# Fused attention and two feed-forward layers on one core: parameters loaded first, GpSimd's data work moved to VectorE and ScalarE, fewer row-sum additions ahead of the matmul

## The chip, the cores and the metric

The kernel runs on one core of one Trainium2 chip. The metric is the device time of one execution in microseconds. The median of three runs before is 496.93 us (496.86 to 497.22).

## The reference

Attention for 2 batches, 12 heads, 448 positions and head size 64, with a soft cap on the scores, followed by two token-wise layers on 896 tokens of width 768:

```python
scores = cap * np.tanh(scale * (q @ k.T) / cap)          # per batch and head
attn = np.exp(scores - scores.max(-1, keepdims=True))
attn = attn / (attn.sum(-1, keepdims=True) + 1e-09)
x = (attn @ v)                                           # then laid out as 896 x 768

h = x @ w_in                                             # 768 -> 2048
P = a[0] + a[1]*h + a[2]*h*h + a[3]*h*h*h
Q = 1.0 + abs(b[0])*abs(h) + abs(b[1])*h*h
x = (P / (Q + 1e-06)) @ w_out                            # 2048 -> 768

h = np.maximum(np.maximum(x @ w1, x @ w2), x @ w3)       # three 768 x 768
out = h @ w_out2                                         # 768 x 768
```

All weights arrive as 64-bit floating-point numbers. The kernel reads their two 32-bit words and makes 32-bit floats of them itself.

## The kernel before, in words

The work runs in stages that overlap at their borders. In the attention stage (about 4 to 94 us) there are six double pairs `d`, each of four heads (two pairs of heads, index `r`). For each double pair TensorE makes seven score tiles: three whole blocks of 128 keys for each `r` (call `scores(d, 0..5)`, line 629), and one tile for the left-over 64 keys of both pairs (`scores(d, 6)`, line 637, which is `scores(d, 2 * NFULL)`). ScalarE takes the tanh of each tile (lines 651 and 654), with a factor `qscale` computed from the parameters, and then the exponential (line 658). TensorE multiplies the exponentials with `v` (lines 682 and 701). For the row sums, VectorE first adds the key blocks of one `r` together (line 723; `ADDED[d]` says how many additions there are, and with 3 it also adds the left-over block on 64 partitions, line 731), and TensorE multiplies what is left with a matrix of ones (line 755). The reciprocals travel through memory and scale the attention output (lines 797 to 805), which is split into a high and a low part.

Every later matmul is done three times: high weight by high data, high by low, low by high. Lines 825, 927, 1075 and 1183 are the matmuls of the first layer up, the first layer down, the second layer (a seven-product scheme with sums of weight blocks made at line 525) and the last one.

Each weight is decoded from its 64-bit words in `decoded()`: step s1 scales the upper words (ScalarE line 457, or another engine at line 460), step s2 makes the three missing bits from the lower words (ScalarE line 465, VectorE line 467), step s4 joins them on VectorE (line 471). When s1 was not done by ScalarE, s4 has a second instruction that puts the sign in (line 475). Then the weight is split into a high part (line 494) and a low part (line 497).

Between up and down each element of `h` passes ScalarE (absolute value line 842, cubic line 845, square line 848), VectorE (lines 851, 854), one addition for the denominator (line 859), ScalarE's logarithm and exponential in place of a division (875, 876), and VectorE again (879, 882, 885, and the split at 899 and 902).

No order is written out by hand. Every operation is put into a list with its cost for each engine that may do it, and `Flow.issue` plays the list through on a model of the engines before the program is built: at each moment an engine takes, among the operations that are ready, the one with the earliest due time. An operation goes to an engine that is not its first only if that is no later than waiting for its first engine, by the costs; `dear` adds to the cost on such an engine. `SPARE` multiplies all costs but TensorE's. The chosen order is fixed in the program, so each engine works through its own list and waits where data is late. All transfers go through one queue, SP's, in the order of due times; `con`, the 4 KB of parameters broadcast to all partitions, had due time 2.0 and so stood behind the transfers of the first two pairs.

Of the kernel before, what the change touches and what calls it, by code (L numbers as in the profile page):

```python
# [18 lines left out]
P = 128  # L19
# [9 lines left out]
QGUARD = 1.0 + 1e-6  # L29
TINY = 1e-30  # L30
LOW = 7.49
JOIN, SIGN = 0.9, 0.87
DEAR = 0.0, 99.0, 1.0
CAP = 6
NG = 6
LAG = 3
# [11 lines left out]
BACKLOG = 14.0, 2.0  # L48

SWITCH, SAME = {"rows": 0.21, "both": 0.16, "halves": 0.16, "quarters": 0.13, None: 0.2}, 6.0  # L50
SPARE = 1.05

TANH = 0.89

# [7 lines left out]

FIRST = 2

ADDED = 3, 3, 3, 3, 3, 3

# [257 lines left out]
def attention_moe(ctx: ExitStack, tc: tile.TileContext, qk, v, w_in, w_out, w123, w_out2, par, out):  # L326
# [74 lines left out]
        return add({"sp": issue}, lambda e: nc.sync.dma_start(out=out_(), in_=in_()), after, vals, size=size, **kw)  # L401


    con_in = dma(lambda: con, lambda: par.broadcast_to([P, 8]), size=0.004, issue=0.45, due=2.0)
    idle = slot("idle", F32R)
    zero = add({"dve": 0.45}, lambda e: dve.memset(f32(two(idle)[:, 0]), 0.0), (), [idle])

# [42 lines left out]
    def decoded(key, src):  # L450
        kn = "".join(str(x) for x in key)
        raw, dec = Val("raw", f"raw{kn}"), slot(f"dec{kn}")

        def scale(e):
            x = f32(raws[raw.at[0]][:, :, 1])
            if e == "act":
                act.activation(flat(dec), x, AF.Prelu, scale=2.0**-112, alpha=-(2.0**32))
                return
            s4.engines["dve"] = (JOIN + SIGN) * SPARE
            engine[e].tensor_scalar(out=flat(dec), in0=x, scalar1=2.0**-112, scalar2=0.0, op0=ALU.mult, op1=ALU.add)  # L460

        def bits(e):
            o = raws[raw.at[0]][:, :, 0]
            if e == "act":
                act.activation(o, raws[raw.at[0]].bitcast(U32)[:, :, 0], AF.Copy, scale=LOW / 2.0**32)  # L465
                return
            dve.tensor_scalar(out=o, in0=o, scalar1=29, scalar2=7, op0=ALU.logical_shift_right, op1=ALU.bitwise_and)

        def join(e):
            t = flat(dec).bitcast(I32)  # L470
            dve.scalar_tensor_tensor(  # L471
                out=t, in0=t, scalar=3, in1=raws[raw.at[0]][:, :, 0], op0=ALU.logical_shift_left, op1=ALU.bitwise_or
            )
            if s1.on != "act":
                dve.scalar_tensor_tensor(
                    out=t, in0=raws[raw.at[0]][:, :, 1], scalar=-0x80000000, in1=t, op0=ALU.bitwise_and,
                    op1=ALU.bitwise_or,
                )

        got = dma(  # L480
            lambda: raws[raw.at[0]].rearrange("p n t -> p (n t)"), lambda: src.bitcast(I32), (), [raw],
            size=0.786, issue=0.5, ahead=AHEAD,
        )
        s1 = add({"act": 0.83, "pool": 0.87, "dve": 0.47}, scale, [got], [raw, dec], leave=LEAVE, ahead=AHEAD)
        s1.dear = {"pool": DEAR[0], "dve": DEAR[1]}
        s2 = add({"act": 0.83, "dve": 0.47}, bits, [got], [raw], shared=True, leave=LEAVE, ahead=AHEAD)
        s2.dear = {"dve": DEAR[2]}
        s4 = add({"dve": JOIN}, join, [s1, s2], [raw, dec], shared=True)
        return dec, s4

    def split(dec, at, n, hi, hat, lo, lat, after):

        def high(e):
            copy_on[e](flat(hi)[:, hat : hat + n], flat(dec)[:, at : at + n])

        def low(e):
            engine[e].tensor_tensor(
                out=flat(lo)[:, lat : lat + n], in0=flat(dec)[:, at : at + n], in1=f32(flat(hi)[:, hat : hat + n]),
                op=ALU.subtract,
            )  # L500

        f = n / DM
        s5 = add({"act": 0.1 + 0.64 * f, "dve": 0.07 + 0.4 * f}, high, after, [dec, hi], shared=True, leave=KEEP, ahead=LATE)
        return add({"dve": 0.06 + 0.82 * f, "pool": 0.1 + 1.7 * f}, low, [s5], [dec, lo, hi], shared=True)

    def weight(key, src):
        w = weights[key] = Weight()
# [6 lines left out]
    def branch_weights(o, m):  # L514
        kn = f"{o}{m}"
        top, t4 = decoded(("m", o, m), w123[o, m])
        bot, b4 = decoded(("m", o + 3, m), w123[o + 3, m])
        sd = slot(f"sd{kn}")
        first, second = slice(0, NH), slice(NH, DM)

        def combine(out_, x, y, op, after):
            (o_, oc), (x_, xc), (y_, yc) = out_, x, y
            return add(
                {"dve": 0.47, "pool": 0.95},
                lambda e: engine[e].tensor_tensor(out=flat(o_)[:, oc], in0=flat(x_)[:, xc], in1=flat(y_)[:, yc], op=op),
                after, [o_, x_, y_], shared=True,
            )

        h1, l1, h2, l2, h3, l3 = (slot(f"m{z}{kn}", F32R) for z in ("h1", "l1", "h2", "l2", "h3", "l3"))
        x4 = slot(f"mx{kn}", F32R)  # L530
        s1 = combine((sd, first), (bot, first), (bot, second), ALU.add, [b4])
        s2 = combine((sd, second), (sd, first), (top, first), ALU.subtract, [s1, t4])
        s3 = combine((bot, first), (top, first), (bot, first), ALU.subtract, [s1, t4])
        d1 = split(top, 0, DM, h1, 0, l1, 0, [t4])
        d3 = split(sd, 0, DM, h3, 0, l3, 0, [s1, s2])
        d2 = split(bot, 0, DM, h2, 0, l2, 0, [s3])
        s4 = combine((top, second), (top, second), (sd, second), ALU.subtract, [d1, s2])
        d4 = split(top, NH, NH, x4, 0, x4, NH, [s4])
        weights["m", o, m] = {
            "A11": (h1, 0, l1, 0, d1), "A12": (h1, NH, l1, NH, d1), "S1": (h3, 0, l3, 0, d3), "S2": (h3, NH, l3, NH, d3),  # L540
            "S3": (h2, 0, l2, 0, d2), "A22": (h2, NH, l2, NH, d2), "S4": (x4, 0, x4, NH, d4),
        }
# [174 lines left out]
    def added(d, r):  # L717
        y, done = slot(f"es{d}_{r}"), None
        for n in range(min(ADDED[d], NFULL - 1)):
            (x, ex, one), (z, ez, other) = (E[d, r * NFULL] if n == 0 else (y, done, lambda: two(y))), E[d, r * NFULL + n + 1]  # L720

            def plus(e, one=one, other=other):
                engine[e].tensor_tensor(out=two(y), in0=one(), in1=other(), op=ALU.add)

            done = add({"dve": 1.0, "pool": 2.1}, plus, [ex, ez, done], [x, y, z], shared=True)
        if ADDED[d] == NFULL:
            x, ex, one = E[d, 2 * NFULL]
            rr = slice(r * D, r * D + D)

            def ends(e):  # L730
                engine[e].tensor_tensor(out=two(y)[rr], in0=two(y)[rr], in1=one()[rr], op=ALU.add)

            done = add({"dve": 1.0, "pool": 2.1}, ends, [ex, done], [x, y], shared=True)
        ADDS[d, r] = y, done, lambda: two(y)

    def summed(d):
# [48 lines left out]
    def scale_pair(d, r, wrote):  # L785
# [4 lines left out]
        for j in range(2):  # L790
# [2 lines left out]
            got.append(dma(lambda rr=rr: rows[row.at[0]][rr], lambda src=src: src, [wrote], [row], size=0.3, issue=0.55))  # L793
        u = lambda: two(xu)[:, r]
        m = add(
            {"dve": 0.54, "pool": 1.1},
            lambda e: engine[e].tensor_tensor(out=u(), in0=u(), in1=rows[row.at[0]], op=ALU.mult),
            [*got, *parts], [xu, row], shared=True,
        )
# [4 lines left out]
        def low(e):  # L804
            engine[e].tensor_tensor(out=two(x)[:, 1], in0=u(), in1=f32(two(x)[:, 0]), op=ALU.subtract)

        X[b, p] = x, add({"dve": 0.54, "pool": 1.1}, low, [hi], [x, xu], shared=True)


    Hh, A, W, T, G, work, readers = {}, {}, {}, {}, {}, {}, {}  # L810
# [1 line left out]
    def up(n):  # L812
# [45 lines left out]
        def denom(e):  # L858
            engine[e].tensor_tensor(out=two(t_)[:, i], in0=two(t_)[:, i], in1=two(a_)[:, i], op=ALU.add)  # L859

        ab = add({"act": 0.5}, absolute, [dep, scal], [h, a_])
        cu = add({"act": 0.63}, cubic, [dep], [h, w_])
        sq = add({"act": 0.5}, square, [dep, rooted], [h, t_])
        p1 = add({"dve": 0.54}, first, [cu], [h, w_])
        p2 = add({"dve": 0.60}, second, [p1], [h, w_])
        de = add({"dve": 0.54, "pool": 1.12}, denom, [ab, sq], [a_, t_], shared=True)
        readers[n] = p2
        work[k] += [p2, de]
        if i == 1:
# [24 lines left out]
    def parts(k):  # L894
        g, dep = G[k]
        hi, lo = slot(f"gh{k}", F32R), slot(f"gl{k}", F32R)

        def high(e):
            copy_on[e](two(hi), two(g))

        def low(e):
            engine[e].tensor_tensor(out=two(lo), in0=two(g), in1=f32(two(hi)), op=ALU.subtract)  # L902

        h_ = add({"act": 0.845, "dve": 0.54}, high, [dep], [g, hi], shared=True)
        l_ = add({"dve": 1.0, "pool": 2.1}, low, [h_], [g, hi, lo], shared=True)
        GH[k], GL[k] = (hi, h_), (lo, l_)

    acc, count = {}, {}
# [45 lines left out]
    def from_slot(name, o, t, i, after):  # L954
# [5 lines left out]
        def low(e):  # L960
            engine[e].tensor_tensor(out=two(x)[:, 1], in0=two(t)[:, i], in1=f32(two(x)[:, 0]), op=ALU.subtract)

        XB[name, o] = x, add({"dve": 0.54, "pool": 1.1}, low, [h_], [t, x], shared=True)
        return XB[name, o][1]

    near, evacuated = {}, {}
# [32 lines left out]
    for d in range(B * ND):  # L999
        for r in range(2):  # L1000
            prep(2 * d + r)
        values(d)
        scores(d, 2 * NFULL)
        if d:
            weighted_rest(d - 1)
        for n in range(NFULL):
            scores(d, 2 * n)
            scores(d, 2 * n + 1)
            if d:
                if n < 2:  # L1010
                    weighted(d - 1, n)
                else:
                    scale(d - 1, summed(d - 1))
# [81 lines left out]
    def branches(n):  # L1095
# [44 lines left out]
        for (oc, i), done in ends.items():  # L1140
# [5 lines left out]
                shared=True,  # L1146
            )
            dones.append((i, add(
                {"dve": 0.54, "pool": 1.1},
                lambda e, hi=hi, lo=lo, r=r, cols=cols, i=i: engine[e].tensor_tensor(  # L1150
                    out=flat(lo, NT)[:, cols], in0=two(r)[:, i], in1=f32(flat(hi, NT)[:, cols]), op=ALU.subtract
                ),
# [105 lines left out]
```

## Time and profile before

| | |
|---|---|
| median of the runs | 496.93 us |
| the profiled execution | 496.0 us, its span 494.2 us |
| TensorE busy | 478.9 us, 97% of the span |
| VectorE busy | 416.1 us, 84% |
| ScalarE busy | 317.9 us, 64% |
| GpSimd busy | 86.9 us, 18%, 75 instructions |
| mean granted TensorE clock | 0.997 |

The span runs from the first to the last instruction of the profiled execution; the time of the execution has 1.8 us around it. PE is TensorE, PEld its weight loads, DVE VectorE, ACT ScalarE, POOL GpSimd, SP the engine that issues the transfers.

### The profile page before, as it was taken

What the parts mean: (1) busy time and instruction counts of PE and PEld (TensorE: products, weight loads), DVE (VectorE), ACT (ScalarE), POOL (GpSimd) and SP (SyncE); (2) the same over time, 40 slices, a digit from 0 to 9 for tenths busy, and PEclk for the clock granted to TensorE, in tenths of its full rate; (3) what the DMA queues carried; (4) which work ended last, traced back from release to release, by engine and by line L of the source; (5) the groups of instructions that cost most, each with busy time, mean ns of one, the idle gap of its engine ahead of it and who ended that gap; (6) DMA issues with size and microseconds to landing.
All of it is one profiled execution on the core that took longest, in us unless ns stands there. A gap on an engine that the chain in (4) does not pass through costs nothing.

```text
span 494.2 us, 6389 instructions
## 1 busy us (share of the span) xinstructions
PE 478.9 (97%) x2410; PEld 394.4 (80%) x2410; DVE 416.1 (84%) x561; ACT 317.9 (64%) x426; POOL 86.9 (18%) x75
## 2 busy tenths in 40 slices
PE   6898999999999999999998999999999999999997
PEld 3332344388899799889997899999999999999997
DVE  0799999999999899999999989876999989997000
ACT  3998999777878958788887646653234442552111
POOL 0241001033321222211130210121313250100000
PEclk9999999999999999999999999999999999999999
DMA  7965521061033131342312666730025053030111
GB/s 260 414 256 177 142 77 38 7 200 37 14 115 129 64 129 64 129 127 85 105 60 89 233 221 234 255 127 2 0 67 188 1 192 118 10 129 32 65 64 65
DMA packets 16591, 58.35 MB, mean 118 GB/s; under 512 B 3608, under 2 KB 7088, under 8 KB 16560
## 3 DMA queue, kind: packets, MB, share of 16 engines
q1 hardware_dynamic: 16560, 57.94, 34.3%
q8 instruction: 19, 0.31, 0.3%
q14 instruction: 12, 0.10, 0.1%
HBM read 55.10 MB, written 2.84 MB: 117 GB/s over the span
## 4 chain that ended last, share of the span: by engine, by line
PE 59%; DVE 22%; ACT 12%; issue 3%; DMA 2%; SPq 1%; POOL 0%; DVEq 0%
PE b L1075 23%; PE b L927 15%; PE b L1183 9%; PE b L825 6%; DVE W L854 2%; PE b L701 2%; DVE T L879 2%; DVE W L851 2%; DMA raw<-in_w_in_dram 2%; ACT A L842 2%; ACT T L848 2%; DVE decin L471 2%; PE bb L629 2%; DVE W L885 2%; DVE gl L902 2%
## 5 line engine op out<-in xcount | busy, mean ns | idle before, releaser
L825 PE MATMUL b<-x,whin 128*128 128x448 f32 x384 | 111.0, 370 | 1.7 <-DVE W L854 1.1
L825 PEld LDWEIGHTS b<-x,whin 128*128 128x128 f32 x384 | 70.9, 188 | 14.1 <-issue 3.4
L825 PE MATMUL b<-x,wlin 128*128 128x448 f32 x192 | 70.3, 366 | 0.0
L1075 PE MATMUL b<-T,mh 128*128 128x448 f32 x216 | 61.3, 365 | 0.0
L465 ACT ACTIVATE raw<-raw 128x768 int32<-128x768 uint32 x46 | 42.0, 918 | 19.2 <-DMA raw<-in_w_dram 9.9
L1075 PEld LDWEIGHTS b<-T,mh 128*128 128x128 f32 x216 | 40.6, 188 | 3.2
L1075 PE MATMUL b<-T,ml 128*128 128x448 f32 x108 | 39.4, 365 | 0.0
L825 PEld LDWEIGHTS b<-x,wlin 128*128 128x128 f32 x192 | 36.1, 188 | 3.0
L927 PE MATMUL b<-gl,whoa 128*128 128x448 f32 x96 | 35.3, 368 | 2.4 <-DVE gl L902 2.4
L658 ACT ACTIVATE e<-e,con 128x2688 f32<-128x2688 f32 (+1 forms) x18 | 37.4, 2122 | 0.0
L859 POOL TENSOR_TENSOR T<-T,A 128x448 f32<-128x448 f32 x17 | 24.2, 1423 | 73.8 <-ACT T L848 73.8
L927 PE MATMUL b<-gh,whob 128*128 128x448 f32 x96 | 35.2, 366 | 0.0
L927 PE MATMUL b<-gh,whoa 128*128 128x448 f32 x96 | 35.1, 366 | 0.0
L927 PE MATMUL b<-gh,wloa 128*128 128x448 f32 x96 | 35.1, 365 | 0.0
L927 PE MATMUL b<-gl,whob 128*128 128x448 f32 x96 | 35.1, 365 | 0.0
L927 PE MATMUL b<-gh,wlob 128*128 128x448 f32 x96 | 35.1, 365 | 0.0
L651 ACT ACTIVATE e<-bb,qscale 128x896 f32<-128x896 f32 x31 | 32.0, 1070 | 0.4 <-PE bb L637 0.3
L1075 PE MATMUL b<-B,mh 128*128 128x448 f32 x108 | 30.6, 365 | 0.0
L701 PE MATMUL b<-e,v 128*64 128x448 f32 x144 | 29.0, 545 | 1.5 <-ACT e L658 1.4
L1198 ACT COPY ob<-b 128x384 f32<-128x384 f32 x13 | 6.3, 482 | 36.2 <-PE b L1183 36.2
L1183 PE MATMUL b<-who,h3l 128*128 128x384 f32 x84 | 28.1, 334 | 0.0
L1183 PE MATMUL b<-who,h3h 128*128 128x384 f32 x84 | 28.1, 334 | 0.0
(157 smaller groups left out, 1119.6 us busy)
## 6 DMA issues: line engine op xcount, KB each, us to landing
raw<-in_w_out_dram SPq DMA_DIRECT2D x22, 768.0 KB, 4.3
raw<-in_w_dram SPq DMA_DIRECT2D x18, 768.0 KB, 4.4
raw<-in_w_in_dram SPq DMA_DIRECT2D x16, 768.0 KB, 7.3
qk<-in_qk_dram SPq DMA_DIRECT2D x11, 448.0 KB, 8.2
v<-in_v_dram SPq DMA_DIRECT2D x6, 448.0 KB, 4.3
row<-rsum SPq DMA_DIRECT2D x24, 112.0 KB, 2.8
out_dram<-ob SPq DMA_DIRECT2D x6, 384.0 KB, 2.7
out_dram<-ob SPq DMA_DIRECT2D x2, 192.0 KB, 1.9
```

Of the source, the lines that this page charges most:

```text
L465: act.activation(o, raws[raw.at[0]].bitcast(U32)[:, :, 0], AF.Copy, scale=LOW / 2.0**32)
L471: dve.scalar_tensor_tensor(out=t, in0=t, scalar=3, in1=raws[raw.at[0]][:, :, 0], op0=ALU.logical_shift_left, op1=ALU.bitwise_or)
L629: pe.matmul(pair(t, j)[:, :S], k[rr], q[rr], start=True, stop=True)
L651: act.activation(view(), twins[t.at[0] // 2][:, :, :S], AF.Tanh, scale=qscale)
L658: act.activation(all_, all_, AF.Exp, scale=cap)
L701: pe.matmul(bank(o)[j * D : j * D + D, :S], whole(vr, n, r, j), view()[:, j], start=False, stop=n == NFULL - 1,)
L825: pe.matmul(bank(h)[:, :S], w_, x_, start=cc == 0 and i == 0, stop=cc == NCC - 1 and i == len(terms) - 1)
L842: act.activation(two(a_)[:, i], bank(h)[:, :S], AF.Abs, scale=b0)
L859: engine[e].tensor_tensor(out=two(t_)[:, i], in0=two(t_)[:, i], in1=two(a_)[:, i], op=ALU.add)
L927: pe.matmul(bank(a)[:, :S], w_, g_, start=count[half, o, b] == 1, stop=count[half, o, b] == 3 * NFC)
L1075: pe.matmul(bank(o)[:, :S], w_, m_, start=cc == 0 and i == 0, stop=cc == 2 and i == 2)
L1183: pe.matmul(bank(o)[:, :NH], h_, w_, start=ocs[0] == 0 and i == 0, stop=ocs[-1] == NCC - 1 and i == len(terms) - 1,)
```

## The change

GpSimd's cost is taken out of every operation that has data to work on, so the planner can give it to VectorE or ScalarE only. `con` gets the earliest due time of all transfers. For step s1 VectorE's extra cost falls from 99 to 3, for step s2 from 1 to 0.5. Some costs are set a little differently (the joining instructions 0.95, the absolute value and the square 0.6, the margin 1.04). In double pairs 0 to 3 two additions are made ahead of the row-sum matmul in place of three, so the left-over keys go through a matmul of their own there. In double pair 0 the score tile of the left-over keys stands behind four whole tiles, not ahead of all.

```diff
-JOIN, SIGN = 0.9, 0.87
-DEAR = 0.0, 99.0, 1.0
+JOIN, SIGN = 0.95, 0.95
+DEAR = 0.0, 3.0, 0.5
-SPARE = 1.05
+SPARE = 1.04
-ADDED = 3, 3, 3, 3, 3, 3
+ADDED = 2, 2, 2, 2, 3, 3
-    con_in = dma(lambda: con, ..., size=0.004, issue=0.45, due=2.0)
+    con_in = dma(lambda: con, ..., size=0.004, issue=0.45, due=-20.0)
-        s1 = add({"act": 0.83, "pool": 0.87, "dve": 0.47}, scale, ...)
+        s1 = add({"act": 0.83, "dve": 0.47}, scale, ...)
...
-        return add({"dve": 0.06 + 0.82 * f, "pool": 0.1 + 1.7 * f}, low, ...)
+        return add({"dve": 0.06 + 0.82 * f}, low, ...)
...
-                {"dve": 0.47, "pool": 0.95},          # combine, line 525
+                {"dve": 0.47},
-            done = add({"dve": 1.0, "pool": 2.1}, plus, ...)
+            done = add({"dve": 1.0}, plus, ...)
...
-        ab = add({"act": 0.5}, absolute, ...)
+        ab = add({"act": 0.6}, absolute, ...)
-        sq = add({"act": 0.5}, square, ...)
+        sq = add({"act": 0.6}, square, ...)
-        de = add({"dve": 0.54, "pool": 1.12}, denom, ...)
+        de = add({"dve": 0.54}, denom, ...)
...
-        scores(d, 2 * NFULL)
         if d:
+            scores(d, 2 * NFULL)
             weighted_rest(d - 1)
         for n in range(NFULL):
             scores(d, 2 * n)
             scores(d, 2 * n + 1)
+            if not d and n == 1:
+                scores(d, 2 * NFULL)
```

The lines with "..." stand for the other operations that lose their GpSimd cost in the same way: the scaling of the attention output and its low part (797, 805), the low part at 902, the low part at 961 and the low part at 1150.

## Rows read from the trace of the kernel before

**Rows 1.** The page's busy times: engine, us, share of the span, instructions.

```profile
PE 478.9 (97%) x2410; PEld 394.4 (80%) x2410; DVE 416.1 (84%) x561; ACT 317.9 (64%) x426; POOL 86.9 (18%) x75
```

**Rows 2.** Stages: from:to, length, busy us per engine, clock, DMA share, GB/s.

```profile
25.00:71.00 46.00, 44.12 (x248) 14.76 (x244) 45.41 (x55) 44.75 (x44) 8.11 (x5) 1.00 0.53 173
71.00:92.00 21.00, 20.63 (x114) 10.49 (x112) 20.91 (x31) 20.72 (x20) 2.01 (x2) 1.00 0.08 24
115.00:266.00 151.00, 147.05 (x714) 132.75 (x712) 143.35 (x171) 122.91 (x172) 33.26 (x22) 1.00 0.27 90
266.00:449.00 183.00, 182.78 (x902) 169.20 (x903) 168.11 (x250) 88.74 (x128) 33.15 (x28) 1.00 0.36 121
332.00:447.00 115.00, 115.00 (x570) 106.56 (x569) 105.99 (x160) 48.42 (x72) 24.81 (x21) 1.00 0.23 80
```

**Rows 3.** Timeline of the start: start us, us, instruction, [idle before, releaser].

```profile
0.73 1.34 SPq L401 DMA_DIRECT2D qk<-in_qk_dram  x3
2.11 0.43 SPq L401 DMA_DIRECT2D con<-in_par_dram  x1
...
4.28 2.89 PE L629 MATMUL bb<-qk 64*128 64x448 f32 x8
7.01 0.92 PE L629 MATMUL b<-qk 64*128 64x448 f32 x4
...
9.10 0.20 ACT L423 ACTIVATE absb<-con 128x2 f32<-128x2 f32 x1 [7.09 <-DMA con<-in_par_dram]
...
9.55 1.91 ACT L651 ACTIVATE e<-bb,qscale 128x896 f32<-128x896 f32 x2
...
10.61 3.08 PE L637 MATMUL bb<-qk 64*64 64x448 f32 x16 [2.69 <-ACT e L651]
```

**Rows 4.** Transfers: destination and source, count, KB each, us to landing.

```profile
comp<-sums SPq DMA_DIRECT2D x6, 7.0 KB, 2.0
...
con<-in_par_dram SPq DMA_DIRECT2D x1, 4.0 KB, 7.0
```

**Rows 5.** What ScalarE waited for on others, 9 to 88 us: us, times, longest.

```profile
ACT absb L423 <- DMA con<-in_par_dram: 7.1, 1, 7.1
...
ACT e L651 <- PE bb L637: 0.3, 1, 0.3
```

**Rows 6.** TensorE's row-sum group, 25 to 71 us: busy us, mean ns | idle before.

```profile
L755 PE MATMUL b<-es,ones 128*32 128x448 f32 x24 | 2.9, 550 | 1.5 <-DVE xu L712 1.5
```

**Rows 7.** GpSimd: the denominators (92 to 266 us); line 460 in two stages.

```profile
L859 POOL TENSOR_TENSOR T<-T,A 128x448 f32<-128x448 f32 x17 | 24.2, 1423 | 73.8 <-ACT T L848 73.8
...
0.00:92.00 92.00, 12.56 (x9) 0.98 0.53 184
92.00:266.00 174.00, 6.21 (x5) 1.00 0.29 95
```

**Rows 8.** VectorE's groups, 0 to 92 us: busy us, mean ns | idle before.

```profile
L723 DVE TENSOR_TENSOR es<-es,e 128x896 f32<-128x896 f32 x12 | 14.4, 1204 | 0.1
...
L731 DVE TENSOR_TENSOR es<-es,e 64x896 f32<-64x896 f32 x11 | 11.9, 1080 | 0.2
L475 DVE SCALAR_TENSOR_TENSOR decin<-raw,decin 128x768 int32<-128x768 int32 x6 | 7.5, 1258 | 0.2
```

**Rows 9.** VectorE's groups, 92 to 266 us.

```profile
L879 DVE SCALAR_TENSOR_TENSOR T<-T,A 128x896 f32<-128x896 f32 x15 | 19.8, 1322 | 0.0
...
L859 DVE TENSOR_TENSOR T<-T,A 128x448 f32<-128x448 f32 x15 | 9.2, 619 | 0.0
...
L797 DVE TENSOR_TENSOR xu<-xu,row 128x448 f32<-128x448 f32 x4 | 3.4, 858 | 0.0
```

**Rows 10.** VectorE lines 879 and 467, whole span: ns shortest/median/longest.

```profile
L879 DVE SCALAR_TENSOR_TENSOR T<-T,A x16: 1075/1084/2739, 112.4 to 268.0; 128x896 f32<-128x896 f32 x16
...
L467 DVE TENSOR_SCALAR raw<-raw x10: 548/556/1293, 14.3 to 313.9; 128x768 int32<-128x768 int32 x10
```

**Rows 11.** ScalarE's step s1, whole span: busy us, mean ns.

```profile
L457 ACT ACTIVATE decin<-raw 128x768 f32<-128x768 f32 x7 | 6.4, 909 | 0.0
```

More of the change, by code (lines that the diff above doesn't have):

```diff
@@ L401, in dma @@
         return add({"sp": issue}, lambda e: nc.sync.dma_start(out=out_(), in_=in_()), after, vals, size=size, **kw)
-    con_in = dma(lambda: con, lambda: par.broadcast_to([P, 8]), size=0.004, issue=0.45, due=2.0)
+    con_in = dma(lambda: con, lambda: par.broadcast_to([P, 8]), size=0.004, issue=0.45, due=-20.0)
     idle = slot("idle", F32R)
@@ L483, in decoded @@
         )
-        s1 = add({"act": 0.83, "pool": 0.87, "dve": 0.47}, scale, [got], [raw, dec], leave=LEAVE, ahead=AHEAD)
+        s1 = add({"act": 0.83, "dve": 0.47}, scale, [got], [raw, dec], leave=LEAVE, ahead=AHEAD)
         s1.dear = {"pool": DEAR[0], "dve": DEAR[1]}
@@ L503, in split @@
         s5 = add({"act": 0.1 + 0.64 * f, "dve": 0.07 + 0.4 * f}, high, after, [dec, hi], shared=True, leave=KEEP, ahead=LATE)
-        return add({"dve": 0.06 + 0.82 * f, "pool": 0.1 + 1.7 * f}, low, [s5], [dec, lo, hi], shared=True)
+        return add({"dve": 0.06 + 0.82 * f}, low, [s5], [dec, lo, hi], shared=True)
     def weight(key, src):
@@ L723, in plus @@
                 engine[e].tensor_tensor(out=two(y), in0=one(), in1=other(), op=ALU.add)
-            done = add({"dve": 1.0, "pool": 2.1}, plus, [ex, ez, done], [x, y, z], shared=True)
+            done = add({"dve": 1.0}, plus, [ex, ez, done], [x, y, z], shared=True)
         if ADDED[d] == NFULL:
@@ L731, in ends @@
                 engine[e].tensor_tensor(out=two(y)[rr], in0=two(y)[rr], in1=one()[rr], op=ALU.add)
-            done = add({"dve": 1.0, "pool": 2.1}, ends, [ex, done], [x, y], shared=True)
+            done = add({"dve": 1.0}, ends, [ex, done], [x, y], shared=True)
         ADDS[d, r] = y, done, lambda: two(y)
@@ L795, in scale_pair @@
         m = add(
-            {"dve": 0.54, "pool": 1.1},
+            {"dve": 0.54},
             lambda e: engine[e].tensor_tensor(out=u(), in0=u(), in1=rows[row.at[0]], op=ALU.mult),
@@ L805, in low @@
             engine[e].tensor_tensor(out=two(x)[:, 1], in0=u(), in1=f32(two(x)[:, 0]), op=ALU.subtract)
-        X[b, p] = x, add({"dve": 0.54, "pool": 1.1}, low, [hi], [x, xu], shared=True)
+        X[b, p] = x, add({"dve": 0.54}, low, [hi], [x, xu], shared=True)
     Hh, A, W, T, G, work, readers = {}, {}, {}, {}, {}, {}, {}
@@ L859, in denom @@
             engine[e].tensor_tensor(out=two(t_)[:, i], in0=two(t_)[:, i], in1=two(a_)[:, i], op=ALU.add)
-        ab = add({"act": 0.5}, absolute, [dep, scal], [h, a_])
+        ab = add({"act": 0.6}, absolute, [dep, scal], [h, a_])
         cu = add({"act": 0.63}, cubic, [dep], [h, w_])
-        sq = add({"act": 0.5}, square, [dep, rooted], [h, t_])
+        sq = add({"act": 0.6}, square, [dep, rooted], [h, t_])
         p1 = add({"dve": 0.54}, first, [cu], [h, w_])
         p2 = add({"dve": 0.60}, second, [p1], [h, w_])
-        de = add({"dve": 0.54, "pool": 1.12}, denom, [ab, sq], [a_, t_], shared=True)
+        de = add({"dve": 0.54}, denom, [ab, sq], [a_, t_], shared=True)
         readers[n] = p2
@@ L904, in parts @@
         h_ = add({"act": 0.845, "dve": 0.54}, high, [dep], [g, hi], shared=True)
-        l_ = add({"dve": 1.0, "pool": 2.1}, low, [h_], [g, hi, lo], shared=True)
+        l_ = add({"dve": 1.0}, low, [h_], [g, hi, lo], shared=True)
         GH[k], GL[k] = (hi, h_), (lo, l_)
@@ L961, in low @@
             engine[e].tensor_tensor(out=two(x)[:, 1], in0=two(t)[:, i], in1=f32(two(x)[:, 0]), op=ALU.subtract)
-        XB[name, o] = x, add({"dve": 0.54, "pool": 1.1}, low, [h_], [t, x], shared=True)
+        XB[name, o] = x, add({"dve": 0.54}, low, [h_], [t, x], shared=True)
         return XB[name, o][1]
@@ L1148, in branches @@
             dones.append((i, add(
-                {"dve": 0.54, "pool": 1.1},
+                {"dve": 0.54},
                 lambda e, hi=hi, lo=lo, r=r, cols=cols, i=i: engine[e].tensor_tensor(
```

## The prediction

> **What bounds the kernel now.** I read the busy times first: TensorE is at 97%, VectorE at 84%, so what can be won lies in the 3% and in what TensorE loses without it showing [rows 1]. The stages say where [rows 2]. From 332 to 447 us TensorE runs 570 matmuls in 115.0 us, 0.2018 us each, and waits for nothing: this is its full rate, and 266 to 449 us keeps it. From 115 to 266 us it runs 714 of the same matmuls, which would take 144.1 us, in 151: some 6.9 us are lost there, with VectorE busy 143.35 of 151. In the attention stage ScalarE is the fullest: 44.75 of 46 us from 25 to 71 and 20.72 of 21 from 71 to 92; TensorE (44.12 and 20.63) and VectorE (45.41 and 20.91) stand beside it, so it is a stage in which three engines are near their ends at once.
>
> The third view is the timeline of the start [rows 3]. TensorE has its first scores from 4.28 us, has made three tiles by 7.93 and stops, having no free bank. ScalarE does nothing on data until 9.10, when the parameters land, and begins its first tanh at 9.55. The transfer of the parameters was issued at 2.11 behind three of q and k, and landed 7.0 us later; a transfer of about the same size (7 KB) that has the queue for itself lands in 2.0 [rows 4]. From then to 88 us ScalarE waits 0.3 us for another engine [rows 5]. So the start of the tanh moves the whole attention stage, as long as nothing else takes its place. That is the reading on which the forecast rests.
>
> **The parameters first.** The three issues took 1.34 us, so the parameters go out at 0.73 in place of 2.11 and with 2.0 us to landing are there at about 2.7; the first q and k move back by their issue, 0.43 us [rows 3, 4]. The first scores then begin at 4.7, and one tile (a third of the 3.65 us from 4.28 to 7.93) is ready at 5.7 to 5.9. The tanh starts there in place of 9.55: 3.7 us earlier. If the landing is 7.0 us again, it is at 7.7, after which the scalars take 0.45: 8.2, 1.4 us earlier. Upper bound: 9.55 - 5.5 = 4.0. Every transfer behind the moved one, the first weights for VectorE included, waits 0.43 us once. I take 3.5, since the second pair's q and k must now be there some 3 us sooner than TensorE asked for them before. The left-over tile of double pair 0 stands later, which needs the second pair later by one tile; in the trace it ran behind three whole tiles anyway, at 10.61, so I give it nothing, between 0 and the 0.3 us that ScalarE waited for it [rows 3, 5].
>
> **The left-over keys.** Each of double pairs 0 to 3 loses two additions on 64 partitions (1.08 us each, eight in all: 8.6 us of VectorE) and gets a second set of row-sum matmuls, eight instructions that take 2.9 / 3 = 0.96 us: 3.85 us of TensorE [rows 6, 8]. The sums of pairs 0 to 2 fall into 25 to 71 us, where TensorE is idle 1.88 us, 1.5 of it before just such a sum, for VectorE [rows 2, 6]. The fourth falls behind 71, where first-layer matmuls fill TensorE's gaps, and costs its 0.96. Hidden: 1.9; paid: 1.9. Bounds: 1.0 (three hidden) and 3.85.
>
> **GpSimd's work in the attention stage.** Up to 92 us it did s1 of nine weights [rows 7]. ScalarE would take 0.909 us for one, and then VectorE is spared the sign instruction [rows 8, 11]; VectorE would take about what its pass over the lower words takes, a median of 0.556 [rows 10]. The planner decides by ScalarE's backlog: with 3 us of extra cost VectorE takes s1 when some 2.6 us of ready work stand before ScalarE. In a stage where ScalarE has no gap, three tiles that wait for their tanh (1.91 us for two [rows 3]) are enough, so I put at most one or two on ScalarE and the rest on VectorE: 9 x 0.56 = 5.0 us. Against it stands what VectorE loses beside GpSimd, read as mean less undisturbed duration: four groups, from the sign instruction, 6 x (1.258 - 0.958), to the second additions, 12 x (1.204 - 1.08), come to 5.5 us [rows 8]. With the 8.6 us from above VectorE has some 8 us more in this stage, 4 after the earlier end of it. This buys decoded weights for the next stage; on the stage itself I count nothing. Bounds: 0, and 8.2 us lost if ScalarE takes all nine.
>
> **The middle stage, 92 to 266 us.** GpSimd's 17 denominators cost VectorE 17 x 0.619 = 10.5 us [rows 7, 9], five smaller operations there 3.9 by the same time per element. Out go eight sign instructions (0.96 each, 7.7 us) if ScalarE, which has 28 us free here, does s1, of which GpSimd did five in this stage [rows 2, 7]. Out goes also the waiting beside GpSimd: line 879 has a median of 1.084 us and a mean of 1.322 over 15, that is 3.6 us, and nine such groups, from this one to line 797 (4 x 0.25), come to 9.5, or 8.7 without the sign instructions [rows 9, 10]. Balance: 14.4 - 7.7 - 8.7 = -2.0 us of VectorE, and 4 us of head start from attention, against the 6.9 us that TensorE loses. A denominator is also ready in 0.62 us and not in 1.42. I take 1.7 us of gain, a quarter of the loss; bounds: 6.9 (all of it) and -5 (below).
>
> The longest instance of line 879, 2.739 us beside a median of 1.084, is 1.65 longer, more than one denominator on GpSimd [rows 7, 10]. The Trainium skill (Perfetto Trace Analysis, Optimizing Scalar/DVE Operations) says that with VectorE saturated it may make sense to offload to ScalarE or even GpSimd, but that GpSimd and VectorE share a port, so that moving work between those two might not help. VectorE is saturated here; by the first half of that sentence the change is wrong, and its outcome is the last rival below; by the second half it loses nothing, which is the sum above. The row of line 879 speaks for the second half.
>
> **Behind 266 us.** Thirteen sums of weight blocks and six low parts come to VectorE (about 11 us) and nine sign instructions go (8.6). VectorE has 15 us free, ScalarE 94, and TensorE loses 0.2 [rows 2]. Nothing, with bounds of 0 and 2 us lost. The cost constants move no instruction by themselves; they alter the order, for which I leave 1 us on either side.
>
> **The sum.** -3.5 + 1.9 + 0 - 1.7 + 0 = -3.3 us. The profiled execution's span of 494.2 becomes 490.9, its time of 496.0 becomes 492.7. It lies 0.9 us under the median of the runs, 496.93, so against that I expect 493.6. What is late next is TensorE itself, as soon as first-layer matmuls can fill its gaps, then VectorE in the middle stage.
>
> **The rivals.**
> *The middle loss goes too.* With VectorE relieved in both stages TensorE runs at full rate from 92 us on, and three sums are hidden: -3.7 + 1.0 - 5.5 = -8.2, 488.7 us. For it speaks that VectorE's waits beside GpSimd are large; against it, that the middle chain also goes through ScalarE, whose work grows there. 0.20.
> *The start does not move as it should.* The parameters land after 7 us again, or the second pair's q and k are late and ScalarE runs dry: -1.4 + 1.9 - 1.7 = -1.2, 495.7 us. For it speaks that the cause of the 7.0 us is not in a row, only the comparison with the lone transfer. 0.13.
> *ScalarE takes s1 in the attention stage.* The planner gives ScalarE each gap it sees, and where GpSimd was free before there is now none. Nine at 0.909 us are 8.2 us on the engine that bounds the stage: -3.3 + 8.2 = +4.9, 501.8 us. It decides from four of them on (3.3 / 0.909). For it: the extra cost of 3 us. Against it: before, ScalarE did not take one s2 there until 88 us, although VectorE's extra cost was 1. 0.14.
> *VectorE saturates in the middle stage.* s1 falls to VectorE (5 x 0.56 = 2.8), the sign instructions stay, and only half of the waiting beside GpSimd comes back: 14.4 + 2.8 - 4.4 = 12.8 us, 5.2 more than the 7.65 us that it has free [rows 2]. -3.5 + 1.9 + 5.2 = +3.6, 500.5 us. It decides as soon as the waiting given back is under some 7 us. 0.08.
>
> **How the numbers follow.** The forecast has 0.45, its own range is 491.0 to 496.3. A measurement can tell about 0.2%, 1.0 us, from no change. Faster: 0.41 of the forecast, 0.20, and half of the second rival, 0.06: 0.67. Same: 0.04, 0.07 and 0.02 of the slower ones: 0.13. Slower: 0.20. The range of 8 in 10 runs from 489.0, which leaves out the better part of the first rival, to 499.0, which leaves out the dear ends of the last two.
>
> **What would show it.** Right: the first tanh at 5.5 to 6.2 us, ScalarE without a gap from there, its last tanh under 84 us; two row-sum sets in four double pairs; line 879 with a mean near 1.09; more than 714 matmuls in 151 us of the middle. Wrong: a first tanh behind 8 us; four or more of line 457 before 85 us; TensorE waiting for q and k; line 475 still at eight in the middle stage, and TensorE losing more than 6.9 us there. If the first layer's matmuls do not begin some 3 us earlier, the step on the start has failed.

## The result and the profile after

The changed kernel takes 491.12 us (median of 4 runs, 490.64 to 494.02), the kernel before 496.89: 5.8 us less, a ratio of 0.9897 (95% interval 0.9858 to 0.9935). The profiled execution has a span of 489.3 us against 494.2, so 4.9 us less; the one of the kernel before, 496.0, lay 0.9 under its median. The direction and the range of the forecast held, its own range (491.0 to 496.3) only just; the gain is 5.8 us by the medians and 4.9 by the spans, and not 3.3.

The stages of the kernel after, as in [rows 2]:

```profile
25.00:71.00 46.00, 46.00 (x278) 17.31 (x276) 44.79 (x66) 45.88 (x45) 0.00 (x0) 1.00 0.52 175
71.00:92.00 21.00, 19.99 (x118) 8.42 (x116) 19.71 (x30) 20.22 (x25) 0.00 (x0) 1.00 0.19 61
...
115.00:266.00 151.00, 148.99 (x725) 135.69 (x726) 142.32 (x187) 118.11 (x165) 0.00 (x0) 1.00 0.22 75
266.00:449.00 183.00, 183.00 (x910) 169.93 (x909) 165.06 (x269) 93.18 (x133) 0.00 (x0) 1.00 0.35 121
```

TensorE runs 725 matmuls in the 151 us of the middle in place of 714: at 0.2018 us each it loses 4.7 us there and not 6.9. It is never idle from 25 to 71. How far it is ahead when the middle begins, the first layer's matmuls up to 115 us tell (line 825, columns as in [rows 2] with TensorE alone). Before, then after:

```profile
0.00:115.00 115.00, 25.37 (x117) 0.99 0.50 173
```

```profile
0.00:115.00 115.00, 27.11 (x128) 1.00 0.55 192
```

That is 11 matmuls, 2.2 us. The start, as in [rows 3]:

```profile
0.73 0.39 SPq L401 DMA_DIRECT2D con<-in_par_dram  x1
...
1.17 2.31 SPq L401 DMA_DIRECT2D qk<-in_qk_dram  x5
...
3.98 0.20 ACT L423 ACTIVATE absb<-con 128x2 f32<-128x2 f32 x1 [1.98 <-DMA con<-in_par_dram]
...
4.96 3.36 PE L629 MATMUL bb<-qk 64*128 64x448 f32 x8 [0.60 <-DMA qk<-in_qk_dram]
...
6.87 1.01 ACT L651 ACTIVATE e<-bb,qscale 128x896 f32<-128x896 f32 x1 [2.36 <-PE bb L629]
...
8.11 1.63 PE L629 MATMUL b<-qk 64*128 64x448 f32 x4
```

The parameters land at 3.98, 3.2 us after their issue and not 7.0 [rows 4]; ScalarE now waits for TensorE's first tile and starts 2.7 us earlier than before. Two of the prediction's signs missed: the first tanh lies behind 6.2 us and ScalarE has a gap of 0.49 us after it. One of its signs of being wrong showed: TensorE waited 0.60 us for q and k. VectorE, 92 to 266 us, by group as in [rows 9], and the sign instruction (line 475) in the attention stage and the middle stage as windows (busy us and count):

```profile
L859 DVE TENSOR_TENSOR T<-T,A 128x448 f32<-128x448 f32 x32 | 19.1, 617 | 0.0
...
L879 DVE SCALAR_TENSOR_TENSOR T<-T,A 128x896 f32<-128x896 f32 x16 | 17.3, 1082 | 0.0
```

```profile
0.00:92.00 92.00, 6.76 (x7) 1.00 0.55 197
92.00:266.00 174.00, 0.00 (x0) 1.00 0.26 88
```

All 32 denominators are VectorE's, line 879 has lost its waits (mean 1.082 us, before 1.322), and no sign instruction is left in the middle stage. A milestone compares the kernels better than windows do: the group of the second layer's matmuls that comes first in every kernel with its shortest, median and longest duration in ns, then first and last start. Before, then after:

```profile
L1075 PE MATMUL b<-T,mh x216: 362/365/369, 333.9 to 442.9; 128*128 128x448 f32 x108
```

```profile
L1077 PE MATMUL b<-T,mh x216: 362/365/370, 329.0 to 438.0; 128*128 128x448 f32 x108
```

It begins 4.9 us earlier, which is the whole gain of the span: behind it nothing changed. Of the 4.9, 2.2 us stand ahead of 115 us, another 2.2 come in the middle stage, and the rest lies between 266 us and the second layer. I call it the second layer's start below. The first layer's first matmul moved from 71.2 to 67.9.

### The profile page after: what moved, and what is told of

The parts are those of the page before. It is cut to its first block, busy times and chain, and to the rows that moved or that the text cites. A ratio compares the mean times of both kernels' runs of the same rounds, so it can differ in the third digit from the quotient of the medians.

```text
span 489.3 us, 6386 instructions
## 1 busy us (share of the span) xinstructions
PE 479.0 (98%) x2442; PEld 396.2 (81%) x2442; DVE 404.0 (83%) x601; ACT 321.6 (66%) x427; POOL 0.9 (0%) x10
## 4 chain that ended last, share of the span: by engine, by line
PE 75%; DVE 10%; ACT 9%; DMA 4%; issue 1%; SPq 0%; DVEq 0%; ACTq 0%
PE b L1077 23%; PE b L927 19%; PE b L825 12%; PE b L1185 9%; PE b L701 4%; PE bb L629 4%; ACT e L658 2%; DVE W L854 2%; DMA row<-rsum 1%; DMA comp<-sums 1%; DVE W L882 1%; DVE W L851 1%; ACT e L651 1%; ACT A L842 1%; ACT T L848 1%; PE b L629 1%
## 5 line engine op out<-in xcount | busy, mean ns | idle before, releaser
L465 ACT ACTIVATE raw<-raw 128x768 int32<-128x768 uint32 x44 | 40.1, 914 | 18.8 <-DMA raw<-in_w_dram 8.6
L1185 PE MATMUL b<-wlo,h3h 128*128 128x384 f32 x84 | 28.1, 334 | 0.0
```

Of the source, the lines that this page charges most:

```text
L1185: pe.matmul(bank(o)[:, :NH], h_, w_, start=ocs[0] == 0 and i == 0, stop=ocs[-1] == NCC - 1 and i == len(terms) - 1,)
```

## The experiments

Every time below is a median beside runs of the kernel before on the same chip (496.8 to 497.3). The runs of one kernel spread over 0.7 to 6 us, so the second layer's start is given too. Where an experiment keeps the order, every engine runs the same instructions one after another as in the kernel that it is made from, but for the edit.

**The parameters fourth again, order kept.**

```diff
 # the changed kernel; the transfer of con is issued ahead of the fourth one of SP
-    con_in = dma(lambda: con, ..., due=-20.0)            # first in the queue
+    (len(issued) == 3 and nc.sync.dma_start(out=con, in_=par.broadcast_to([P, 8])), ...)
```

> The changed kernel with its order on every engine kept, but the parameters' transfer put back behind the first three of q and k. Theory (the start carries some 3 us of the gain by timing alone): the parameters land near 9 us, the first tanh starts near 9.5 in place of 6.87, and the time rises by 2.4 to 3.3 us, to 493.5 to 494.4. Rival (the gain comes from the newly planned order, the start is absorbed by slack in the attention stage): under 1 us, below 492.1.

493.93 us (ratio 0.992, 0.989 to 0.995), 2.8 above the changed kernel. The interval reaches into that of the changed kernel, so the time alone doesn't settle it; the trace does:

```profile
9.87 1.91 ACT L651 ACTIVATE e<-bb,qscale 128x896 f32<-128x896 f32 x2
...
10.93 3.36 PE L629 MATMUL bb<-qk 64*128 64x448 f32 x8 [3.03 <-ACT e L651]
```

```profile
L1077 PE MATMUL b<-T,mh x216: 362/365/369, 332.7 to 441.8; 128*128 128x448 f32 x108
```

The first tanh is 3.0 us later than after, and the second layer's start 3.7: in the new order the start is handed on whole.

**The parameters first, the rest as before.** The same edit the other way, order kept.

```diff
 # the kernel before; the transfer of con is issued ahead of the first one of SP
-    con_in = dma(lambda: con, ..., due=2.0)              # fourth in the queue
+    (len(issued) == 0 and nc.sync.dma_start(out=con, in_=par.broadcast_to([P, 8])), ...)
```

> The kernel before with its order on every engine kept, but the parameters' transfer issued first. Theory: the first tanh starts near 6.9 in place of 9.55 and the time falls by 2.4 to 3.3 us, to 493.6 to 494.5; with the run that undoes it in the changed kernel the two differences agree within 1 us. Rival (VectorE, full from 14 us on, holds the attention stage back in the old order): under 1 us, above 495.9.

495.30 us (0.9971, 0.9947 to 0.9995), 1.8 below the kernel before, though the first tanh starts at 6.5, 3 us earlier. The second layer's start, 334.1, did not move in the profiled execution, which is one of the three longest of twelve (498.44). The theory's number failed here: on the old order the attention stage takes most of the earlier start back. That is the rival's place for the loss, though the time fell by more than its 1 us. ScalarE now waits for TensorE there, in three groups, 5.7 us from 6 us on:

```profile
ACT e L651 <- PE bb L629: 3.1, 3, 2.0
ACT row L767 <- PE b L755: 1.5, 1, 1.5
ACT e L651 <- PE bb L637: 1.1, 1, 1.1
```

Without the wait for the first tile (2.0) that is 3.7 us, where before it waited 0.3 for a tile [rows 5]. The last tanh starts at 82.7, only 0.7 us earlier than before (83.4), and the first layer at 70.4 in place of 71.2. VectorE is as full as before from 25 to 71 us (45.42 us of 46), while TensorE and ScalarE are less so (42.75 and 43.50); that the full VectorE is the cause fits this, but no run shows it.

**GpSimd and the constants as before.**

```diff
 # the changed kernel
-JOIN, SIGN = 0.95, 0.95        DEAR = 0.0, 3.0, 0.5       SPARE = 1.04
+JOIN, SIGN = 0.9, 0.87         DEAR = 0.0, 99.0, 1.0      SPARE = 1.05
-        ab, sq: {"act": 0.6}
+        ab, sq: {"act": 0.5}
+ and "pool" with its cost in every operation that had it
```

> The changed kernel with GpSimd's costs and all cost constants as before, so that the planner gives GpSimd data work again; parameters first, two additions and the moved score tile stay. Theory (middle stage gains by VectorE's relief from waits beside GpSimd and from sign instructions): 1.5 to 2.5 us slower than the changed kernel, 492.6 to 493.6, with line 879 at a mean over 1.25 us and TensorE losing more in the middle stage. Rival (offloading to GpSimd helps a saturated VectorE): faster than 490.5. Second rival (the removal did nothing either way): within 0.7 us of 491.1.

496.40 us (0.9976, 0.9949 to 1.0004): 5.3 above the changed kernel, more than twice what I expected, and hardly below the kernel before. Its middle stage, and line 879 from 92 to 266 us, which waits again as expected:

```profile
115.00:266.00 151.00, 146.24 (x710) 131.98 (x709) 142.24 (x171) 116.60 (x163) 35.34 (x22) 1.00 0.19 70
```

```profile
L879 DVE SCALAR_TENSOR_TENSOR T<-T,A 128x896 f32<-128x896 f32 x16 | 20.2, 1264 | 0.0
```

710 matmuls in place of 725; the second layer starts at 333.3. This is the part that carries most. It joins two things, GpSimd's work and the constants; a kernel with GpSimd's costs and the new constants was not run.

**Three additions again.**

```diff
-ADDED = 2, 2, 2, 2, 3, 3
+ADDED = 3, 3, 3, 3, 3, 3
```

> The changed kernel with three additions ahead of the row sums in all six double pairs, planned anew. Theory (TensorE pays about half of its 3.85 us in the attention stage, VectorE has room since GpSimd is out of its way): 1 to 2 us faster, 489.1 to 490.1. Rival (VectorE's 8.6 us in the attention stage are worth as much or more): the same or slower, 491.1 to 493.

491.53 us (0.9877, 0.9845 to 0.9910): the same as the changed kernel, as the rival said. The first layer begins at 70.6, 2.7 us later than after, but by 115 us TensorE has run as many of its matmuls (127, after 128), and the second layer begins at 329.2. So what TensorE saves in row sums, 3.85 us by the prediction's price, is gone by then; VectorE's 8.6 us of additions stand beside it.

**Every second denominator by GpSimd, order kept.**

```diff
-            engine[e].tensor_tensor(out=two(t_)[:, i], ...)
+            (pool if n % 2 else dve).tensor_tensor(out=two(t_)[:, i], ...)
```

> The changed kernel, its order kept on every engine, with every second denominator of the middle stage (16 of 32) done by GpSimd in place of VectorE. VectorE is spared some 16 x 0.6 = 9.6 us. Theory A (what VectorE is spared it loses again in waits beside GpSimd, and a denominator comes later): line 879 has single instances over 2 us again, TensorE loses 1 to 4 us more in the middle stage, 492 to 495. Theory B (a saturated VectorE gains from what is taken off it): 488.5 to 490.5. Theory C (neither matters): within 0.7 us of 491.1.

493.54 us (0.9918, 0.9885 to 0.9950), 2.4 above; the second layer starts at 331.5, 2.5 later. First the middle stage, then groups of GpSimd and of VectorE from 92 to 266 us:

```profile
115.00:266.00 151.00, 146.07 (x712) 133.00 (x712) 138.94 (x171) 117.10 (x163) 23.29 (x14) 1.00 0.22 73
```

```profile
L859 POOL TENSOR_TENSOR T<-T,A 128x448 f32<-128x448 f32 x16 | 25.8, 1611 | 229.4 <-ACT T L848 229.4
```

```profile
L879 DVE SCALAR_TENSOR_TENSOR T<-T,A 128x896 f32<-128x896 f32 x16 | 18.8, 1176 | 0.0
...
L859 DVE TENSOR_TENSOR T<-T,A 128x448 f32<-128x448 f32 x16 | 10.9, 678 | 0.0
```

VectorE was spared some 14 x 0.6 = 8.4 us in that window, and its busy time fell by 3.4 (142.32 to 138.94): most of the rest came back as longer instructions, and a denominator on GpSimd took 1.6 us in the mean. Line 879 has an instance of 2.06 us again. Theory A, by its trace.

The Trainium skill (Perfetto Trace Analysis, Optimizing Scalar/DVE Operations) leaves both open, that offloading from a saturated VectorE to GpSimd may make sense and that it might not help because the two share a port; here it did not help (493.54 us against 491.12).

**Eight sign instructions more, order kept.**

```diff
-            if s1.on != "act":
+            if s1.on != "act" or (key[0] == "in" and key[1] >= 8):
```

> The changed kernel, its order kept, with the sign instruction done once more for the eight last weights of the up layer, where ScalarE has already put the sign in: 8 x 0.96 = 7.7 us of VectorE in the middle stage, as many as stood there before the change. Theory A (VectorE is the engine that makes TensorE lose time there, so its work counts): 2 to 5 us slower, 493 to 496. Theory B (VectorE's 8.7 us of idle time there take it in): under 1 us, below 492.1.

497.69 us (1.0020, 0.9992 to 1.0048), 6.6 above the changed kernel for 7.7 us of VectorE; the second layer starts at 333.8, 4.8 later. All of the gain is gone.

```profile
115.00:266.00 151.00, 143.91 (x696) 129.62 (x695) 143.40 (x188) 116.62 (x161) 0.00 (x0) 1.00 0.20 68
```

TensorE loses 151 - 696 x 0.2018 = 10.5 us there, 5.8 more than after, and VectorE's busy time rises by only 1.1, since less of its other work falls into the window: its 8.7 us without work could not be used.

**All constants as before, GpSimd out.**

```diff
-JOIN, SIGN = 0.95, 0.95        DEAR = 0.0, 3.0, 0.5       SPARE = 1.04
+JOIN, SIGN = 0.9, 0.87         DEAR = 0.0, 99.0, 1.0      SPARE = 1.05
-        ab, sq: {"act": 0.6}
+        ab, sq: {"act": 0.5}
```

> The changed kernel with all cost constants as before (extra costs 99 and 1, joining 0.9 and 0.87, margin 1.05, absolute value and square 0.5), GpSimd still without data work, planned anew. s1 then falls to ScalarE alone. Theory A (the gain of the GpSimd part is the lost waits and sign instructions, not the constants): within 1.5 us of 491.1, and even less of line 475. Theory B (without VectorE as a way out s1 takes the place of the tanh on ScalarE): 493 to 499, with seven more of line 457 before 85 us.

496.58 us (0.9974, 0.9951 to 0.9998): theory B's time, but not its mechanism: ScalarE did three of line 457 by 85 us, and the last tanh of line 651 began at 79.5, no later than after (80.6). VectorE stood still: 29.5 us busy from 25 to 71, and the first layer began at 79.3.

**Only VectorE's extra cost for s1 as before.**

```diff
-DEAR = 0.0, 3.0, 0.5
+DEAR = 0.0, 99.0, 0.5
```

> The changed kernel with one constant put back, VectorE's extra cost for s1 (99 in place of 3), planned anew. Theory A (with GpSimd out, VectorE has to be allowed to do s1 in the attention stage, or decoded weights are missing later): as slow as with all constants put back, 495 to 498, VectorE busy under 35 us from 25 to 71, three weights decoded by 85 us in place of seven. Theory B (one of the other constants was it): within 1.5 us of 491.1.

495.82 us (0.9972, 0.9942 to 1.0001): this one number is what was missing. The attention stage, then VectorE's groups up to 90 us:

```profile
25.00:71.00 46.00, 45.94 (x290) 15.79 (x286) 30.47 (x43) 45.49 (x47) 0.00 (x0) 1.00 0.33 102
```

```profile
L723 DVE TENSOR_TENSOR es<-e 128x896 f32<-128x896 f32 x12 | 13.1, 1090 | 12.4 <-ACT e L658 12.4
...
L471 DVE SCALAR_TENSOR_TENSOR decin<-decin,raw 128x768 int32<-128x768 int32 x3 | 2.9, 958 | 0.0
```

With ScalarE full and GpSimd gone, hardly any s1 is done there: VectorE decodes three weights by 90 us where after it has decoded seven by 85. The work left over costs time in three places behind. By 115 us TensorE has run 120 of the first layer's matmuls, after 128; its middle stage is 1.0 us short of the one after, and then it waits once more:

```profile
115.00:266.00 151.00, 148.71 (x720) 134.00 (x719) 145.40 (x192) 128.07 (x178) 0.00 (x0) 1.00 0.28 96
266.00:449.00 183.00, 181.56 (x897) 167.75 (x896) 167.85 (x272) 89.96 (x127) 0.00 (x0) 1.00 0.35 121
```

**Nine matmuls on zeros at the start, order kept.**

```diff
-        for _ in range(WARM):
+        for _ in range(WARM + 2):
```

> The changed kernel, its order kept, with nine matmuls on zeros at the start in place of seven, so that TensorE has no gap of 0.6 us before q and k land. Theory A (that gap keeps the first tiles at the lower rate, 1.5 us a tile in place of 0.75): tiles two to four come 0.7 us apart, ScalarE's gaps behind the first tanh go, 0.5 to 2 us faster, 489.1 to 490.6. Theory B (the first tiles are slow for another reason, and the start is limited by ScalarE anyway): within 0.5 us of 491.1.

491.12 us (0.9878, 0.9838 to 0.9918): no difference, as theory B has it. The first tanh came at 6.4.

**The parameters by ScalarE's queue, order kept.**

```diff
-    con_in = dma(lambda: con, ...)                       # SP
+    nc.scalar.dma_start(out=con, in_=par.broadcast_to([P, 8]))
```

> The changed kernel, its order kept, with the parameters' transfer issued by ScalarE's own queue, so that q and k go out 0.43 us earlier on SP's. Theory A (the start is worth its time one for one): the first scores at 4.5 and the first tanh at 6.4 or earlier, 0.3 to 0.8 us faster, 490.3 to 490.8. Theory B (the parameters then land later beside q and k): the first tanh at 8 us or later, 492 to 494.

491.07 us (0.9894, 0.9852 to 0.9936): no difference. The parameters took 4.5 us to land and the first tanh started at 6.2. Neither theory: the first scores began at 5.1, no earlier than after, and what is won at the first tanh is too little to be seen in the time.

**The denominator without VectorE.**

```diff
-        act.activation(two(a_)[:, i], bank(h)[:, :S], AF.Abs, scale=b0)
-        act.activation(two(t_)[:, i], bank(h)[:, :S], AF.Square, scale=root)
-        engine[e].tensor_tensor(out=two(t_)[:, i], in0=two(t_)[:, i], in1=two(a_)[:, i], op=ALU.add)
+        act.activation(two(a_)[:, i], bank(h)[:, :S], AF.Abs, scale=root)
+        act.activation(two(t_), two(a_), AF.Square, bias=lin)      # lin = b0 / (2 root)
-        act.activation(two(a_), two(t_), AF.Ln, bias=qone)
+        act.activation(two(a_), two(t_), AF.Ln, bias=koff)         # koff = QGUARD - lin * lin
```

> The changed kernel with the denominator made without VectorE: one plus |b0 h| plus |b1| h squared is written as the square of (root |h| + c) plus a constant, so the 32 additions of line 859 go and ScalarE's squares become 16 of double length; planned anew. It holds where |b1| is not near zero. VectorE loses 19.1 us of work in the middle stage. Theory A (a microsecond of VectorE there is a microsecond of the kernel until TensorE is full): 3 to 6 us faster, 485 to 488, the middle stage's 151 us hold more than 735 matmuls. Theory B (what remains lost there is ScalarE's and the attention stage's): under 1 us, above 490.1.

486.41 us (0.9778, 0.9750 to 0.9807), 4.7 below the changed kernel and 10.8 below the one before. The middle stage, and the second layer's start:

```profile
115.00:266.00 151.00, 151.00 (x747) 139.96 (x746) 139.45 (x175) 117.00 (x152) 0.00 (x0) 1.00 0.29 100
```

```profile
L1076 PE MATMUL b<-T,mh x216: 362/365/369, 323.5 to 432.5; 128*128 128x448 f32 x108
```

TensorE now loses nothing in the middle: 747 matmuls in 151.00 us. With this the stage is won to its end. ScalarE has less to do as well (313.3 us busy in place of 321.6), so this run alone doesn't tell VectorE's part from ScalarE's.

**Both of the last two.**

```diff
 # the kernel without the additions of line 859
-    con_in = dma(lambda: con, ...)                       # SP
+    nc.scalar.dma_start(out=con, in_=par.broadcast_to([P, 8]))
```

> The kernel without the 32 additions, with the parameters' transfer issued by ScalarE's queue as well. If both work for themselves, the sum of the two: another 0.3 to 0.8 us below the kernel without the additions alone. If the first is hidden, the same as that one.

486.03 us (0.9775, 0.9743 to 0.9807): the same as the last within its interval.

## Why the prediction was right, and what it mis-sized

**The parameters first.** Foreseen 3.5 us, bounds 1.4 and 4.0. The first tanh moved by 2.7 us in the profiled execution; in the experiments that have the parameters first in SP's queue it starts between 5.95 and 6.9, so by 2.7 to 3.6 us earlier than before. In the new order undoing it costs 2.8 us of time and 3.7 us of the second layer's start; in the old order the time fell by 1.8 us, and in the trace the second layer kept nothing of it. The mechanism is the one foreseen, with the new order as its condition. The landing took 3.2 us, between my 2.0 and 7.0, and was hidden behind q and k, which were late by more than their issue: TensorE waited 0.60 us for them. The larger part of what is missing is the first tile: from its start at 4.96 to the tanh it took 1.9 us, where I had 1.2 at most. With eight sign instructions more, a kernel whose start has the same instructions, it took 1.1:

```profile
4.88 1.77 PE L629 MATMUL bb<-qk 64*128 64x448 f32 x8 [0.52 <-DMA qk<-in_qk_dram]
...
5.95 1.91 ACT L651 ACTIVATE e<-bb,qscale 128x896 f32<-128x896 f32 x2 [1.38 <-PE bb L629]
```

**The left-over keys.** Foreseen 1.9 us paid. Undoing the step changes the time by 0.4 us upward, within the intervals, so the term is mis-sized by about 2 us; the sum is off by 2.5. TensorE does run the second set of row sums in double pairs 0 to 3, but VectorE's 8.6 us of additions are worth about as much in a stage where three engines are full. I had counted them as decoded weights and gave them no time.

**GpSimd's work in the attention stage.** As foreseen VectorE did s1 (seven, 0.55 us each) and ScalarE one before 85 us. The rival in which ScalarE takes s1 did not come, and the two runs with the extra cost at 99 show that it would not come in that form: the tanh keeps its place by its due time, and the decoding waits. I wrote that the cost constants move no instruction by themselves and left 1 us for them. That step was wrong: one of them is worth 4.7 us (495.82 against 491.12), by idle time of VectorE in the attention stage, most of which is paid for later.

**The middle stage.** "I take 1.7 us of gain, a quarter of the loss." In the trace TensorE gains 2.2 us in the window from 115 to 266, so by place the term is near. The pieces were right: the eight sign instructions are gone, line 879 is at 1.082 us, ScalarE does all of s1. But undoing the GpSimd part, constants included, costs 5.3 us, since it also bears on the stage ahead of this one and on the time behind it. What I lacked was the price of a microsecond of VectorE in the middle. The run with eight sign instructions gives it: 7.7 us more cost 4.8 us at the second layer's start, 5.8 in the window and 6.6 of time, so 0.6 to 0.9 us each. My own balance, 2.0 us there and 4 us of head start, comes at that price to 3.7 to 5.1 us; this was worked out afterwards, and how much of the 5.3 us is VectorE's relief and how much the one constant is not separated. I took VectorE's 7.65 us without work in [rows 2] for room. Most of it, 6.9 us, is time in which VectorE waits for ScalarE, so before, from 115 to 266 us:

```profile
DVE W L854 <- ACT T L848: 3.2, 7, 1.0
DVE W L854 <- ACT A L842: 1.3, 3, 0.7
DVE W L882 <- ACT A L876: 0.8, 2, 0.7
DVE W L851 <- ACT T L848: 0.8, 2, 0.7
DVE W L851 <- ACT W L845: 0.6, 2, 0.3
DVE W L851 <- ACT A L842: 0.2, 1, 0.2
```

The work added with the sign instructions did not fit into such time. For the same reason the saturation rival's point (waits given back under some 7 us) was set too low: without that room it decides while more than 7 us are still given back.

**The sum.** The parts overlap: undone one at a time they cost 2.8, 0.4 and 5.3, together 8.5, for a gain of 5.8. Start, additions and moved tile without the GpSimd part give 0.7 us (496.40 against 497.12), and the start alone 1.8. What an earlier start brings depends on the stages behind it being able to take it. That the sum came near is in part luck: the start brought less than its term, the left-over keys cost nothing in place of 1.9, and 0.9 of the 5.8 us is the distance of one execution from the median. The order is planned anew with each of these edits, so single numbers of the runs that don't keep it hold the luck of a new order too, of a size that these runs don't show. The moved score tile was not tried by itself, nor were the other constants one at a time.

## What to carry to other kernels

An engine that is 95% busy in a stage and shows a few idle microseconds there may have no room, as VectorE had none here: price its work by one run that adds a known amount with the order kept, before summing a change from small pieces. When an engine is taken out of a planner's choices, look at who may do the first step of each chain of its work, since the cost that keeps an engine from it can leave the chain unstarted. And what is first needed by the fullest engine, however small, belongs first in the queue; whether the earlier start lasts, the same edit made on both kernels tells.

## What the runs showed of the hardware

TensorE's clock. Before, TensorE stood still from 7.93 to 10.61 us for want of a bank, and the granted clock was then at the lower of its two levels (0.50 of 2.4 GHz is 1.2). Stages of before, columns as in [rows 2]:

```profile
10.00:12.00 2.00, 1.39 (x8) 0.50 (x12) 0.00 (x0) 2.00 (x4) 0.01 (x1) 0.50 1.04 432
12.00:14.00 2.00, 2.00 (x14) 0.55 (x8) 0.00 (x0) 1.68 (x3) 0.00 (x0) 0.65 1.01 420
```

and after:

```profile
10.00:12.00 2.00, 2.00 (x16) 0.89 (x15) 0.00 (x0) 2.00 (x4) 0.00 (x0) 1.00 0.99 411
12.00:14.00 2.00, 2.00 (x18) 0.65 (x20) 1.39 (x3) 2.00 (x4) 0.00 (x0) 1.00 1.05 427
```

The two left-over tiles took 3.08 us then and 1.83 now. I had not counted that. It may help the earlier start to last; no run shows it by itself. With the parameters fourth again TensorE stood still for 3.03 us, and its granted clock was again 0.50 from 10 to 14 us.

The first tiles can be slow without that. After, the first two took 3.36 us, with eight sign instructions more 1.77, on the same instructions. The granted clock is 1.00 in both. From 5 to 6 us after, then there:

```profile
5.00:6.00 1.00, 1.00 (x4) 0.59 (x6) 0.00 (x0) 0.00 (x0) 0.00 (x0) 1.00 0.98 387
```

```profile
5.00:6.00 1.00, 1.00 (x6) 0.56 (x8) 0.00 (x0) 0.05 (x1) 0.00 (x0) 1.00 0.95 387
```

With nine matmuls on zeros they took 2.07 us. The cause stays open.

The second layer also has two speeds. In the profiled executions of three experiments, the second, the one with nine matmuls on zeros and the one with ScalarE's queue, each of its matmuls takes 368 ns where others show 362 to 370, and the stage lasts 111.2 us in place of 109.0. The second experiment's group:

```profile
L1075 PE MATMUL b<-T,mh x216: 368/368/368, 334.1 to 445.3; 128*128 128x448 f32 x108
```

The last two have the changed kernel's order, so the order is not the cause, and the granted clock is 1.00 in both cases. The three executions lie 2.4 to 3.6 us above the medians of their kernels (498.44, 494.73 and 493.50 us), so it may be part of the spread between runs of one kernel; that was not tried, and the cause stays open.
